# The lead of a fused attention and mixture-of-experts kernel: the first block's loads and work issued ahead of all later ones, six more staging places, four products of a block in one place

## The chip, the cores and the metric

The kernel runs on one NeuronCore of a Trainium2 chip. The metric is the device time of one launch in microseconds (us), the median of several runs. The engines are named as in the profile: PE (TensorE, matrix products and transposes), DVE (VectorE), ACT (ScalarE), POOL (GpSimd) and SP (SyncE), which in this kernel issues every DMA. Each engine works through its own instructions strictly in the order in which the program lists them.

## The reference

Pooled attention feeds a mixture of four experts, and that feeds a gated pair of products:

```
# q, k, v: (4, 8, 576, 64); 8 keys (values) are averaged to one: 72 per head
k_p = k.reshape(B, H, Sp, pool, D).mean(axis=3)
v_p = v.reshape(B, H, Sp, pool, D).mean(axis=3)
scores = scale * np.matmul(q, k_p.transpose(0, 1, 3, 2))
scores = scores - np.max(scores, axis=-1, keepdims=True)
attn = np.exp(scores)
attn = attn / (np.sum(attn, axis=-1, keepdims=True) + 1e-09)
attn_out = np.matmul(attn, v_p)                 # -> x: (2304, 512)
# experts, E = 4, p = normalised domain_probs
out += p[:, e:e + 1] * (np.maximum(x @ w1[e], 0.0) @ w2[e])
# tail
h = (x @ w1) * (x @ w2) @ w3;  result = h @ w_out
```

All of it is in float32; the big products are made of three products of a high and a low part of each operand.

## The kernel before

**Blocks and tiles.** The 2304 tokens are 18 tiles of 128 rows (t) and 6 blocks of 384 (i). Attention works by tile, the experts by block. The expert part is a sequence of units: unit n of expert 0 and block 0 makes one of 8 chunks of the hidden layer (`expert_h`: 12 products called `g<-xl,w1h`, `g<-xh,w1l`, `g<-xh,w1h` in the profile), and two units later its second product follows (`g<-hhl,w2h` and so on). Attention for blocks 1 to 5 is spread between the units: `hooks[n]` is a list of pieces, and `between(n)` runs it after the first (even n) or the second (odd n) half of a unit.

**The lead.** Before unit 0 stands the list `lead`: everything that block 0 needs. In it, `do_k(0)` pools the keys of batch 0 (`kp` on DVE, `kb` on POOL), `do_qT(t)` transposes the queries of tiles 0 to 2 on PE, `do_scores` and `do_exps` make the exponentials `e`, `do_normalise` divides them (on POOL for tiles 0 and 1), `do_v(0, ...)` pools the values of the 8 heads (three POOL additions for a head, except head 2, which DVE does), `do_turn` transposes the attention weights (`at_ps`, copied by ACT), and `do_attend(0)` is four pieces, hp = 0 to 3, each making two heads of x (`x_ps`), which ACT and DVE split into `xh` and `xl`. `warm(n)` is n transposes without use. `k1` and `kT1` stand for the pooling and the transposition of the keys of batch 1, which tile 4 is the first to need.

**Loads and places.** A load of q, k or v needs a staging place (`spots`); there are 14 of the kind "one", cut out of the tiles `stxh` and `stxl`, of which the six in `lead_only` are used once and the others come back when their content is used up, and two of the kind "wide", for queries of later tiles (`load_qb`, 4 or 8 DMAs for a tile). The list `loads` holds all loads in the order of their use. `fetch()` goes through it and issues each load for which a place is free, passing over those that find none; it runs before every piece. Weights come through a stream of four buffers, `raw`. All these DMAs stand in one queue, SP's, in the order of issue. `dp` is a table of 2304 x 4 numbers that is loaded in pieces of 16 bytes.

**Banks.** In the lead, PSUM banks are taken in turn from eight; afterwards `bank` alternates between two, q2 and q3, for scores, transposes and the like, and `g1_bank` between q0 and q1, for the first products of the experts and, in blocks 1 to 5, for `x_ps`.

Of the kernel before, what the change touches and what calls it, by code (L numbers as in the profile page):

```python
# [8 lines left out]
F32 = mybir.dt.float32  # L9
# [8 lines left out]
def fused_kernel(  # L18
# [24 lines left out]
    B, H, S, D = q.shape  # L43
# [3 lines left out]
    E, _, F = moe_w1.shape  # L47
    P = 128
# [3 lines left out]
    TPB = BLK // P  # L52
# [4 lines left out]
    NP = H // 2  # L57
    NROW = H * NK
    NCH = (NROW + P - 1) // P
# [4 lines left out]
    def segments(t0, n):  # L64
        done = 0
        while done < n:
            b, s = divmod(t0 + done, S)
            step = min(n - done, S - s)
            yield done, step, b, s
            done += step  # L70

    LAG = 2
    LEAD = 3
# [6 lines left out]
    acc_a = experts.enter_context(tc.tile_pool(name="acc_a", bufs=NB // 2))  # L80
# [10 lines left out]
    def bank_q(n, name):  # L91
        return ps_q.tile([P, 512], F32, tag=f"q{n}", name=name)
# [6 lines left out]
    def g1_bank(name):  # L99
        g1_turn[0] += 1  # L100
        return bank_q(g1_turn[0] % 2, name)[:, :BLK]
# [14 lines left out]
    def hi_lo(hi, lo, src, lo_eng=None):  # L116
        nc.scalar.activation(hi, src, AF.Copy)  # L117
        (lo_eng or nc.vector).tensor_tensor(lo, src, hi.bitcast(F32), op=ALU.subtract)  # L118
# [146 lines left out]
    with tc.manual_schedule():  # L265
# [12 lines left out]
        def bank(name):  # L278
            turn[0] += 1
            return spare[(turn[0] - 1) % len(spare)](name)  # L280
# [10 lines left out]


        staging = [xpool.tile([P, 3, 512], F32, tag=t, name="st" + t) for _ in range(3) for t in ("xh", "xl")]
        lead_only = [st[:, n, :] for st in staging[4:] for n in range(3)]
        spots = {"wide": [st[:, :2, :] for st in staging[:2]],
                 "one": lead_only + [st[:, n, :] for st in staging[2:4] for n in range(3)] + [st[:, 2, :] for st in staging[:2]]}
        holds = {}
# [1 line left out]
        def kind_of(what):  # L299
            return "wide" if what[0] == "qb" else "one"  # L300
# [75 lines left out]
        def make_qT(t):  # L376

            if t < LEAD:
                r = in_t.pop(("q", t))
                pt = bank("qT_ps")  # L380
                for hp in range(NP):
                    nc.tensor.transpose(pt[:, hp * P:(hp + 1) * P], r[:, hp * P:(hp + 1) * P], ident)
                qT = acc_a.tile([P, NP, P], F32, tag="acc", name="qT")
                nc.scalar.activation(qT.rearrange("p a b -> p (a b)"), pt, AF.Copy)
            else:
                qT = ap.tile([P, NP, P], F32, tag="qT", name="qT", bufs=1)
                nc.vector.transpose(qT.rearrange("p h (j a) -> p h a j", a=4), in_t.pop(("qb", t)))
            qT_t[t] = qT
# [50 lines left out]
        def attend(i, hp):  # L439
            if hp == 0:  # L440
                x_t[i] = tuple(xpool.tile([P, KC, BLK], F32R, tag=t, name=t) for t in ("xh", "xl"))
            xh, xl = x_t[i]
            px = g1_bank("x_ps") if i else bank("x_ps")
            for off, n, b, s in segments(i * BLK, BLK):
                for a in range(2):
                    nc.tensor.matmul(px[a * D:(a + 1) * D, off:off + n], vp_t[b][:NK, 2 * hp + a],  # L446
                                     at_t[i, hp // 2][:NK, 2 * (hp % 2) + a, off:off + n], start=True, stop=True)
            hi_lo(xh[:, hp, :], xl[:, hp, :], px[:, :BLK])

        loads = []  # L450

        def fetch():
            for what in list(loads):
                if spots[kind_of(what)]:
                    loads.remove(what)
                    {"q": load_q, "qb": load_qb, "k": load_k, "v": load_v}[what[0]](*what[1:])
# [7 lines left out]
        def do_k(b):  # L464
            return [(("k", b, c), lambda c=c: pool_k(b, c)) for c in range(NCH)]

        def do_kT(b):
            return [(None, lambda: make_kT(b, 0, 4)), (None, lambda: make_kT(b, 4, NCH))]
# [4 lines left out]
        def do_qT(t):  # L473
            return [(("q" if t < LEAD else "qb", t), lambda: make_qT(t))] if t < NTILE else []

        def do_scores(t):
            return [(None, lambda: scores(t))]

        def do_exps(t):
            return [(None, lambda: exps(t))]  # L480
# [4 lines left out]
        def do_turn(t):  # L485
            return [(None, lambda half=half: attn_T(t, half)) for half in range(2)]

        def do_attend(i):
            return [(None, lambda hp=hp: attend(i, hp)) for hp in range(NP)]
# [15 lines left out]
        def weight(eng):  # L505
            return [(None, lambda: stream.split(eng))]

        VE, GP = nc.vector, nc.gpsimd
        W0, W1, W2 = 14, 20, 14

        def warm(n):

            def f():
                pw = bank("warm")
                for _ in range(n):
                    nc.tensor.transpose(pw[:, :P], ident, ident)
            return [(None, f)]

        k0, kT0, k1, kT1 = do_k(0), do_kT(0), do_k(1), do_kT(1)
        v0 = do_v(0, GP, GP, VE, GP, GP, GP, GP, GP)  # L520
        lead = (warm(W0) + k0[:4] + kT0[:1] + k0[4:] + do_qT(0) + kT0[1:] + do_qT(1) + do_scores(0) + do_exps(0) + v0[:2]
                + do_qT(2) + do_scores(1) + v0[2:3] + do_exps(1) + do_scores(2) + v0[3:5] + do_normalise(0) + do_exps(2)
                + v0[5:6] + do_normalise(1) + warm(W1) + do_turn(0) + do_normalise(2, VE) + v0[6:]
                + warm(W2) + do_turn(1) + weight(GP) + k1[:2] + do_turn(2) + do_qT(3) + do_attend(0) + weight(VE))

        hooks = [[] for _ in range(2 * FC * ATT_BLOCKS + 4)]
        hooks[0] = k1[2:]
        hooks[1] = do_qT(TPB + 1)
        hooks[2] = kT1
        hooks[3] = [(None, probs)]  # L530
        hooks[5] = [(None, probs_T)]
        for t in range(TPB, NTILE + 1):
            h = hooks[3 * (t - TPB) + (t > TPB):]
            if t < NTILE:
                h[0] += do_scores(t) + do_exps(t)
                if t > TPB:
                    h[1] += do_qT(t + 1)
                one, two = do_normalise(t)
                h[1].append(one)
                h[2].append(two)  # L540
            if t > TPB:
                one, two = do_turn(t - 1)
                h[1].insert(0, one)
                h[2].insert(0, two)
                if t % TPB == 0:
                    for n, piece in enumerate(do_attend(t // TPB - 1)):
                        h[2 + n].append(piece)
        for b, at_v, at_k in ((1, 3, None), (2, 15, 11), (3, 26, 23)):
            for n, piece in enumerate(do_v(b, GP)):
                hooks[at_v + n].append(piece)  # L550
            if at_k:
                for n, piece in enumerate(do_k(b)):
                    hooks[at_k + n // 2].append(piece)
                hooks[at_k + 4] += do_kT(b)
        loads += [what for what, _ in lead + sum(hooks, []) if what]


        acc_t, x2_t, p_t = {}, {}, {}
# [316 lines left out]
                    add_w1(0, m)  # L875
            add_w2(0, n)
        dp = ap.tile([P, NTILE, E], F32, tag="dp", name="dp", bufs=1)
        fetch()
        stream.fill()
        nc.sync.dma_start(dp, domain_probs.rearrange("(t p) e -> p t e", p=P))  # L880
        for piece in lead:
# [71 lines left out]
        for half in range(2):  # L953
            for b in range(B):
# [24 lines left out]
                first, second = xo_t[0], xo_t[1]  # L979
# [95 lines left out]
```

## Time and profile before

| what | value |
|---|---|
| median of 3 runs | 1238.67 us (1236.69 to 1238.8) |
| profiled execution: span | 1235.0 us |
| PE busy | 1207.5 us (98%) |
| DVE, POOL, ACT busy | 666.8, 369.0, 276.3 us |
| DMA over the span | 137.28 MB on SP's queue, 112 GB/s on average |

The span is what the trace covers, from the first instruction to the last; the device time of a run has some microseconds more around it. The busy shares are averages over very different stages: the first 53 us, where block 0 is prepared, look nothing like the rest.

### The profile page before, as it was taken

To read this page: it belongs to the slowest core of one execution; us is meant where nothing else is said; L and a number is where in the kernel's file an instruction comes from. 1 tells how busy PE (TensorE), PEld (TensorE's weight loads), DVE (VectorE), ACT (ScalarE), POOL (GpSimd) and SP (SyncE) were. 2 spreads that over 40 slices of the span, in tenths; PEclk is the share of its full clock that TensorE was granted. 3 is DMA by queue.
4 is the path that set the end of the run, shared out by engine and by line. 5 is a ranking of instruction groups with operands and counts; after the bars stand their busy time and mean duration, and the time that the engine had idled before them with its cause. 6 is when DMAs were issued, how large, how long until landed. Compare 5 with 4: busy or idle time off the path is not lost.

```text
span 1235.0 us, 18786 instructions
## 1 busy us (share of the span) xinstructions
PE 1207.5 (98%) x7089; PEld 1151.8 (93%) x7089; DVE 666.8 (54%) x1489; ACT 276.3 (22%) x535; POOL 369.0 (30%) x432
## 2 busy tenths in 40 slices
PE   6899999999999999999999999999998999999997
PEld 5788898999999999999999999999987999999996
DVE  5777543444445446544434544444288778775453
ACT  3343331122111113111112211111253332231010
POOL 4664410034222117322124622112422222342111
PEclk9899999999999999999999999999999999999998
DMA  7853101134122235322114422222365343944642
GB/s 186 200 154 113 53 11 46 58 111 128 58 48 59 58 74 149 77 48 52 48 51 121 131 71 65 84 84 88 90 208 214 123 172 130 352 152 179 219 153 68
DMA packets 147758, 138.47 MB, mean 112 GB/s; under 512 B 48524, under 2 KB 114644, under 8 KB 147668
## 3 DMA queue, kind: packets, MB, share of 16 engines
q1 hardware_dynamic: 147668, 137.28, 36.6%
q8 instruction: 55, 0.90, 0.3%
q14 instruction: 35, 0.29, 0.1%
HBM read 96.05 MB, written 41.19 MB: 111 GB/s over the span
## 4 chain that ended last, share of the span: by engine, by line
PE 87%; DVE 5%; DMA 3%; issue 1%; POOL 1%; ACT 1%; SPq 1%; DVEq 0%; POOLq 0%; ACTq 0%
PE g L112 23%; PE g L113 23%; PE g L114 23%; PE s L112 5%; PE s L114 5%; PE s L113 5%; PE x_ps L446 1%; PE at_ps L434 1%; PE sc L400 1%; DMA stxl<-in_v_dram 1%; DVE w3hl L118 1%; DVE kp L332 1%; DMA stxh<-in_v_dram 1%; DVE s L651 1%; DMA half<-half 0%
## 5 line engine op out<-in xcount | busy, mean ns | idle before, releaser
L572 DVE SCALAR_TENSOR_TENSOR hhl<-g,hhh 128x384 fp32r<-128x384 f32 x192 | 106.6, 555 | 361.0 <-ACT hhh L571 360.9
L112 PE MATMUL g<-xl,w1h 128*128 128x384 f32 x768 | 262.4, 342 | 0.0
L113 PE MATMUL g<-xh,w1l 128*128 128x384 f32 x768 | 260.7, 339 | 0.0
L112 PE MATMUL g<-hhl,w2h 128*128 128x384 f32 x768 | 260.2, 339 | 0.2 <-DVE part L592 0.2
L114 PE MATMUL g<-xh,w1h 128*128 128x384 f32 x768 | 260.2, 339 | 0.0
L113 PE MATMUL g<-hhh,w2l 128*128 128x384 f32 x768 | 258.1, 336 | 0.0
L114 PE MATMUL g<-hhh,w2h 128*128 128x384 f32 x768 | 258.1, 336 | 0.0
L571 ACT ACTIVATE hhh<-g 128x384 fp32r<-128x384 f32 x192 | 94.4, 492 | 580.2 <-PE g L114 539.4
L224 POOL TENSOR_TENSOR dtmp<-dtmp 128x256 f32<-128x256 f32 x80 | 58.9, 736 | 408.4 <-DVE dtmp L223 365.2
L112 PEld LDWEIGHTS g<-xl,w1h 128*128 128x128 f32 x768 | 145.1, 189 | 4.9 <-issue 2.0
L112 PEld LDWEIGHTS g<-hhl,w2h 128*128 128x128 f32 x768 | 144.3, 188 | 5.0 <-issue 4.0
L113 PEld LDWEIGHTS g<-xh,w1l 128*128 128x128 f32 x768 | 145.0, 189 | 0.0
L114 PEld LDWEIGHTS g<-xh,w1h 128*128 128x128 f32 x768 | 144.9, 189 | 0.0
L113 PEld LDWEIGHTS g<-hhh,w2l 128*128 128x128 f32 x768 | 144.5, 188 | 0.0
L114 PEld LDWEIGHTS g<-hhh,w2h 128*128 128x128 f32 x768 | 144.2, 188 | 0.0
L118 POOL TENSOR_TENSOR g<-c,g 128x576 fp32r<-128x576 f32 x32 | 47.4, 1481 | 193.7 <-ACT g L117 178.2
L593 POOL TENSOR_TENSOR acc<-acc,part 128x384 f32<-128x384 f32 x72 | 71.1, 1019 | 72.0 <-DVE part L592 72.0
L112 PE MATMUL s<-xol,wh 128*128 128x288 f32 x308 | 91.2, 296 | 0.0
L114 PE MATMUL s<-xoh,wh 128*128 128x288 f32 x308 | 91.1, 296 | 0.0
L113 PE MATMUL s<-xoh,wl 128*128 128x288 f32 x308 | 90.6, 294 | 0.0
L112 PEld LDWEIGHTS s<-xol,wh 128*128 128x128 f32 x308 | 57.9, 188 | 0.4 <-DVE half L1011 0.2
L113 PEld LDWEIGHTS s<-xoh,wl 128*128 128x128 f32 x308 | 57.9, 188 | 0.2
(141 smaller groups left out, 1756.8 us busy)
## 6 DMA issues: line engine op xcount, KB each, us to landing
raw<-in_moe_w_dram SPq DMA_DIRECT2D x64, 256.0 KB
din<-in_moe_w_dram SPq DMA_DIRECT2D x64, 256.0 KB
p<-p SPq DMA_DIRECT2D x24, 192.0 KB
acc<-acc SPq DMA_DIRECT2D x6, 768.0 KB
xr<-acc SPq DMA_DIRECT2D x16, 288.0 KB
half<-ob SPq DMA_DIRECT2D x18, 256.0 KB
half<-half SPq DMA_DIRECT2D x18, 256.0 KB
out_dram<-half SPq DMA_DIRECT2D x18, 256.0 KB
```

The costliest lines, as they stand in the source:

```text
L112: nc.tensor.matmul(ps, lh, rl, start=first, stop=False)
L113: nc.tensor.matmul(ps, ll, rh, start=False, stop=False)
L114: nc.tensor.matmul(ps, lh, rh, start=False, stop=last)
L118: (lo_eng or nc.vector).tensor_tensor(lo, src, hi.bitcast(F32), op=ALU.subtract)
L224: nc.gpsimd.tensor_tensor(a, a, b, op=ALU.add)
L332: nc.vector.tensor_reduce(kp[:n], r[:n, :].rearrange("p (r d) -> p d r", d=D), axis=AX.X, op=ALU.add)
L400: nc.tensor.matmul(sc[off:off + n, (hp % 2) * W:(hp % 2 + 1) * W], qT[:, hp, off:off + n], kT_t[b][:, hp * W:(hp + 1) * W], start=True, st ...
L434: nc.tensor.transpose(pt[:NK, g * P:(g + 1) * P], e[:, half * G + g, :], ident)
L446: nc.tensor.matmul(px[a * D:(a + 1) * D, off:off + n], vp_t[b][:NK, 2 * hp + a], at_t[i, hp // 2][:NK, 2 * (hp % 2) + a, off:off + n], sta ...
L571: nc.scalar.activation(hh, ps, AF.Relu)
L572: nc.vector.scalar_tensor_tensor(hl, ps, 0.0, hh.bitcast(F32), op0=ALU.max, op1=ALU.subtract)
L593: nc.gpsimd.tensor_tensor(acc_t[i][:, c], acc_t[i][:, c], part, op=ALU.add)
```

## The change

It has five parts. (1) `first` lists block 0's own loads, and they stand ahead of all others in `loads`; the first `fetch` issues only these. (2) Three tiles of the pool that later holds the experts' sums lend six more places (`stacc`); the third tile holds the transposed queries of tiles 0 to 2. (3) The first two pooling pieces of batch 1's keys and the transposition of tile 3's queries move behind `do_attend(0)` and a weight split. (4) The other three pooling pieces move from `hooks[0]`, where they stood ahead of tile 3's scores, to `hooks[1]`; the last transposition of those keys goes from `hooks[2]` to `hooks[3]`. (5) A later block's four `attend` pieces, one in each of four hooks, stand together in `h[3]`, and the first two of them take their bank from `bank`.

```diff
+        acc_lead = [acc_a.tile([P, 3, 512], F32, tag="acc", name="stacc") for _ in range(3)]
-        lead_only = [st[:, n, :] for st in staging[4:] for n in range(3)]
+        lead_only = [st[:, n, :] for st in staging[4:] + acc_lead[1:] for n in range(3)]
...
-                qT = acc_a.tile([P, NP, P], F32, tag="acc", name="qT")
+                qT = acc_lead[0][:, t, :].rearrange("p (a b) -> p a b", b=P)
...
-            px = g1_bank("x_ps") if i else bank("x_ps")
+            px = g1_bank("x_ps") if i and hp >= 2 else bank("x_ps")
...
-        def fetch():
-            for what in list(loads):
+        def fetch(most=None):
+            for what in loads[:most]:
...
-                + warm(W2) + do_turn(1) + weight(GP) + k1[:2] + do_turn(2) + do_qT(3) + do_attend(0) + weight(VE))
+                + warm(W2) + do_turn(1) + weight(GP) + do_turn(2) + do_attend(0) + weight(VE) + k1[:2] + do_qT(3))
...
-        hooks[0] = k1[2:]
-        hooks[1] = do_qT(TPB + 1)
-        hooks[2] = kT1
-        hooks[3] = [(None, probs)]
+        hooks[1] = k1[2:] + do_qT(TPB + 1)
+        hooks[2] = kT1[:1]
+        hooks[3] = kT1[1:] + [(None, probs)]
...
-                    for n, piece in enumerate(do_attend(t // TPB - 1)):
-                        h[2 + n].append(piece)
+                    h[3] += do_attend(t // TPB - 1)
...
-        loads += [what for what, _ in lead + sum(hooks, []) if what]
+        first = [("k", 0, c) for c in range(NCH)] + [("q", t) for t in range(LEAD)] + [("v", 0, h) for h in range(H)]
+        loads += first + [what for what, _ in lead + sum(hooks, []) if what and what not in first]
...
-        fetch()
+        fetch(len(first))
```

The lists below show the order of instructions on three engines. On SP, from the start of the program, before (`in_k`, `in_q`, `in_v` are the inputs; a q tile is 128x8x64, a tile of later queries 4 times 32x4x224 or 8 times 16x4x224):

```order
L317 DMA stxl<-in_k_dram 64x512
L360 DMA stxl<-in_q_dram 128x8x64
L360 DMA stxh<-in_q_dram 128x8x64
L322 DMA stxh<-in_v_dram 72x512 x2
L360 DMA stxl<-in_q_dram 128x8x64
L322 DMA stxl<-in_v_dram 72x512 x2
L322 DMA stxh<-in_v_dram 72x512
L322 DMA stxl<-in_v_dram 72x512
L372 DMA stxh<-in_q_dram 32x4x224 x4
L372 DMA stxl<-in_q_dram 16x4x224 x8
L137 DMA raw<-in_moe_w_dram 128x4x128 x3
L135 DMA raw<-in_moe_w_dram 128x512
```

Behind these stand `dp`, the values of heads 6 and 7 and the keys of batch 1. And with the change, from the same row on:

```order
L318 DMA stxl<-in_k_dram 64x512
L361 DMA stxl<-in_q_dram 128x8x64
L361 DMA stacc<-in_q_dram 128x8x64 x2
L323 DMA stacc<-in_v_dram 72x512 x4
L323 DMA stxh<-in_v_dram 72x512 x3
L323 DMA stxl<-in_v_dram 72x512
L137 DMA raw<-in_moe_w_dram 128x4x128 x3
L135 DMA raw<-in_moe_w_dram 128x512
L880 DMA dp<-in_moe_domain_probs_dram 128x18x4
L318 DMA stxl<-in_k_dram 128x512 x2
L373 DMA stxh<-in_q_dram 32x4x224 x4
L318 DMA stxh<-in_k_dram 128x512
```

All eight heads' values now stand ahead of the 12 DMAs of later queries, the four weight buffers and `dp`; tile 2's queries went from behind the second head to ahead of the first, and the keys of batch 1 stay behind `dp`.

On DVE, from the end of the lead to tile 3's exponentials (`kp` pools keys of batch 1, `qT` is tile 3's transposition, `xl` and `w1l` the low parts of x and of a weight, `hhl` that of a unit's hidden chunk, `mx` and `e` the maximum and difference of tile 3's scores), before:

```order
L332 TENSOR_REDUCE kp<-stxh 128x64
L332 TENSOR_REDUCE kp<-stxl 128x64
L387 STREAM_TRANSPOSE qT<-stxh 128x4x4x32
L118 TENSOR_TENSOR xl<-x_ps,xh 128x384 x4
L118 TENSOR_TENSOR w1l<-raw,w1h 128x512
L572 SCALAR_TENSOR_TENSOR hhl<-g_433,hhh 128x384
L118 TENSOR_TENSOR w1l<-raw,w1h 128x512
L332 TENSOR_REDUCE kp<-stxl 128x64 x2
L332 TENSOR_REDUCE kp<-stxh 64x64
L412 TENSOR_REDUCE mx<-sc 128x4
L413 TENSOR_TENSOR e<-sc,mx 128x288
```

and with the change:

```order
L118 TENSOR_TENSOR xl<-x_ps,xh 128x384 x4
L118 TENSOR_TENSOR w1l<-raw,w1h 128x512
L333 TENSOR_REDUCE kp<-stxl 128x64 x2
L388 STREAM_TRANSPOSE qT<-stxh 128x4x4x32
L572 SCALAR_TENSOR_TENSOR hhl<-g_429,hhh 128x384
L118 TENSOR_TENSOR w1l<-raw,w1h 128x512
L413 TENSOR_REDUCE mx<-sc 128x4
L414 TENSOR_TENSOR e<-sc,mx 128x288
L413 TENSOR_REDUCE mx<-sc 128x4
L414 TENSOR_TENSOR e<-sc,mx 128x288
L333 TENSOR_REDUCE kp<-stxh 128x64
L333 TENSOR_REDUCE kp<-stxl 128x64
```

The same instructions stand there; two poolings and tile 3's transposition went from ahead of `xl` to behind the weight split, three poolings from ahead of tile 3's scores to behind them.

On ACT, where block 1's x is made some six units later (`xh` is x's high part, `at` the copied attention weights, g_949 and g_963 the hidden chunk of the same unit), before:

```order
L117 ACTIVATE xh<-x_ps 128x384 x2
L414 ACTIVATE e<-e 128x288 x2
L571 ACTIVATE hhh<-g_949 128x384
L117 ACTIVATE w2h<-raw 128x512
L437 ACTIVATE at<-at_ps 72x4x128
L117 ACTIVATE xh<-x_ps 128x384
L437 ACTIVATE at<-at_ps 72x4x128
L117 ACTIVATE xh<-x_ps 128x384
```

and with the change:

```order
L117 ACTIVATE xh<-x_ps 128x384 x4
L415 ACTIVATE e<-e 128x288 x2
L571 ACTIVATE hhh<-g_963 128x384
L117 ACTIVATE w2h<-raw 128x512
L438 ACTIVATE at<-at_ps 72x4x128 x2
```

The four pieces follow one another without other work between them, ahead of the next tile's exponentials.

## Rows read from the trace of the kernel before

**Rows 1.** The page: busy time of the engines.

```profile
PE 1207.5 (98%) x7089; PEld 1151.8 (93%) x7089; DVE 666.8 (54%) x1489; ACT 276.3 (22%) x535; POOL 369.0 (30%) x432
```

**Rows 2.** Windows: start:end, length, busy PE, PEld, DVE, ACT, POOL; clock, DMA share, GB/s.

```profile
0.00:30.20 30.20, 20.71 (x125) 16.38 (x125) 15.62 (x29) 11.50 (x22) 13.79 (x33) 1.00 0.78 182
30.20:37.10 6.90, 5.85 (x13) 3.42 (x14) 5.39 (x8) 1.01 (x2) 4.16 (x9) 0.51 0.93 236
...
43.90:47.30 3.40, 3.27 (x13) 2.96 (x12) 3.33 (x7) 2.53 (x7) 1.04 (x1) 0.50 0.67 171
...
53.00:240.00 187.00, 186.16 (x1150) 169.63 (x1149) 104.88 (x217) 58.99 (x123) 63.25 (x104) 1.00 0.28 80
```

**Rows 3.** Timeline of PE: start, duration, work, [idle before, releaser].

```profile
14.32 0.66 PE L382 MATMUL qT_ps<-ident,stxl 128*128 128x128 f32 x4 [0.63 <-DMA stxl<-in_q_dram]
...
23.37 2.19 PE L434 MATMUL at_ps<-ident,e 128*72 128x128 f32 x16 [0.18 <-POOL e L425]
26.17 2.16 PE L446 MATMUL x_ps<-at,vp 72*64 72x384 f32 x12 [0.61 <-ACT at L437]
31.18 3.15 PE L446 MATMUL x_ps<-at,vp 72*64 72x384 f32 x4 [2.86 <-POOL vp L355]
34.26 0.69 PE L112 MATMUL g<-xl,w1h 128*128 128x384 f32 x1
...
37.75 1.14 PE L400 MATMUL sc<-kT,qT 128*128 128x144 f32 x8
...
43.52 1.30 PE L341 MATMUL kT_ps<-ident,kb 128*128 128x128 f32 x5 [2.52 <-DVE e L413]
44.48 0.67 PE L112 MATMUL g<-xl,w1h 128*128 128x384 f32 x1
...
51.95 0.60 PE L434 MATMUL at_ps<-ident,e 128*72 128x128 f32 x4 [0.41 <-DVE e L413]
```

**Rows 4.** Timeline of SP's DMA issues: start, time until the last is issued, transfer.

```profile
15.10 5.28 SPq L372 DMA_DIRECT2D stxl<-in_q_dram  x8
...
22.54 0.43 SPq L880 DMA_DIRECT2D dp<-in_moe_domain_probs_dram  x1
23.09 3.77 SPq L322 DMA_DIRECT2D stxh<-in_v_dram  x2
```

**Rows 5.** Timeline of POOL: values of heads 0, 3, tile 1's division, head 6, one key product.

```profile
11.62 0.72 POOL L353 TENSOR_TENSOR stxh<-stxh 72x256 f32<-72x256 f32 x1 [1.20 <-DMA stxh<-in_v_dram]
...
16.15 0.72 POOL L353 TENSOR_TENSOR stxl<-stxl 72x256 f32<-72x256 f32 x1 [1.28 <-DMA stxl<-in_v_dram]
...
22.17 1.15 POOL L425 TENSOR_TENSOR e<-e,sm 128x576 f32<-128x576 f32 x1
29.49 0.72 POOL L353 TENSOR_TENSOR stxh<-stxh 72x256 f32<-72x256 f32 x1 [6.17 <-DMA stxh<-in_v_dram]
...
41.69 0.40 POOL L333 TENSOR_TENSOR kb<-kp,mk 128x128 f32<-128x128 f32 x1 [0.49 <-DVE kp L332]
```

**Rows 6.** Timeline of DVE: from head 2's values to tile 3's exponentials.

```profile
15.11 1.04 DVE L351 TENSOR_REDUCE vp<-stxl 72x64 f32<-72x512 f32 x1 [0.19 <-DMA stxl<-in_v_dram]
...
30.71 1.02 DVE L332 TENSOR_REDUCE kp<-stxh 128x64 f32<-128x512 f32 x1 [6.34 <-DMA stxh<-in_k_dram]
...
33.53 1.92 DVE L118 TENSOR_TENSOR xl<-x_ps,xh 128x384 fp32r<-128x384 f32 x4
...
38.47 0.56 DVE L572 SCALAR_TENSOR_TENSOR hhl<-g,hhh 128x384 fp32r<-128x384 f32 x1 [2.37 <-ACT hhh L571]
...
42.45 0.44 DVE L412 TENSOR_REDUCE mx<-sc 128x4 f32<-128x288 f32 x1
...
43.78 0.46 DVE L413 TENSOR_TENSOR e<-sc,mx 128x288 f32<-128x288 f32 x1
```

**Rows 7.** Timeline of DVE, where block 1's first two parts of x are split.

```profile
74.22 0.55 DVE L118 TENSOR_TENSOR xl<-x_ps,xh 128x384 fp32r<-128x384 f32 x1
74.69 2.03 DVE L332 TENSOR_REDUCE kp<-stxh 128x64 f32<-128x512 f32 x2
```

## The prediction, made before the run

> **What bounds the kernel now.** I read the page first: PE is busy 98% of the span [rows 1], so time can only be won where PE stands idle or runs slowly. The windows show where that is [rows 2]: up to 30.2 us PE works 20.71 us (much of it warming up), and from 53 to 240 us it idles only 0.84 of 187 us. So a microsecond saved before 53 us is kept, and one saved later has nearly nothing to come from. In the timeline of PE three things stand out in the lead [rows 3]: the last of four products for x (`x_ps`) waits 2.86 us for pooled values; the first product of unit 0 starts at 34.26; and the transposition of batch 1's keys waits 2.52 us. After either wait the granted clock falls to half (0.51 from 30.2 to 37.1, 0.50 from 43.9 to 47.3), which is 1.2 GHz [rows 2].
>
> The first wait leads to SP. POOL stands idle 6.17 us until head 6 lands, at 29.49 [rows 5]. Its DMA was issued at 23.09, behind the 12 DMAs of later queries (the last 8 alone took 5.28 us to issue), the weights and `dp` [rows 4].
>
> The second wait is put down to DVE's difference `e` [rows 3]. DVE works without a stop from 38.47 to 44.24 (43.78 + 0.46) [rows 6], and the keys' transposition needs the banks that tile 3's scores hold until then. So between the last `xl` (33.53 + 1.92 = 35.45) and 44.24 it is DVE's list of work, not PE, that sets the pace. At 51.95 PE once more waits 0.41 us for an `e` [rows 3].
>
> **The change, part by part.** *The lead up to x.* Heads 6 and 7 now stand right behind head 5. Head 3 lands at 16.15 and head 2 was in use at 15.11 [rows 5, 6], so a head takes about 1.04 us, and heads 4 to 7 are in by some 20.3. POOL then sets the start of x. From head 0 (11.62) to the end of tile 1's division (22.17 + 1.15 = 23.32) it needed 11.70 us, 1.28 of them idle for head 3 [rows 5]: 10.42 us of work, five heads at 1.62 and two divisions.
>
> But tile 2's queries now land ahead of head 0. Before, head 1 and these queries took from 11.62 to 14.32 together, 2.70 us [rows 3, 5]; a head takes 0.79 (14.32 to 15.11 [rows 3, 6]) to 1.04, so the queries cost 1.66 to 1.91. I take 1.9: head 0 at 13.5, the division's end at 23.92, 0.6 later than before. The bounds: if the queries cost nothing, POOL waits for head 3 as before (23.32); if head 0 comes only when the queries came, 14.32, the end is 24.74.
>
> PE began x 2.85 us after the division (26.17 against 23.32) and needs 0.72 for each pair of heads (2.16 for three) [rows 3]: start 26.77, end 29.65 instead of 34.33. Heads 6 and 7 are pooled by 23.92 + 2 x 1.62 = 27.2, and the fourth product needs them at 28.93, so that wait is gone with 1.7 us to spare. The last `xl` ended 1.12 us after the last product (35.45 against 34.33 [rows 3, 6]): now 30.77, 4.68 earlier. The first weight's low part, which POOL makes behind head 7, takes about as long as a division, so it is there by 28.5.
>
> *From x to tile 3.* Here something is given back. The two poolings and the transposition of tile 3, which DVE did while it waited for x (30.71 to 33.53, 2.82 us [rows 6]), now come behind `xl`. DVE needed 8.79 us from 35.45 to 44.24, of which 2.37 were a wait for unit 0's `hhh` [rows 6]. That wait is filled: 8.79 - 2.37 + 2.82 = 9.24, so the three poolings that are now last end at 30.77 + 9.24 = 40.01, and DVE is **4.23 us** ahead of before (44.24).
>
> The new wait is at tile 3's scores: their transposition ends about 0.65 (a weight split) + 2.82 after 30.77, at 34.2, while unit 0's 12 products, begun at 29.65, last at most the 3.49 us they took at half clock (34.26 to 37.75 [rows 3]). PE idles 1.1 us or more; behind it stand the products of units 1 and 2. Nobody on DVE waits for these until DVE reaches unit 1's `hhl`, behind the poolings, so the wait is hidden under DVE's list; without that cover it would cost its 1.1 to 2.5 us. The order "scores before keys" moves no work, but the keys' transposition now waits for the last pooling and POOL's product of 0.40 [rows 5] instead of for `e`: 40.01 + 0.5 + 0.1 = 40.6 for unit 2's first product, 3.9 ahead of 44.48. From there PE needed 7.06 us to the next stop (51.95 - 0.41) [rows 3]: 47.7. DVE, 4.23 ahead, releases that stop at 47.7 too. So 4.2 us are won at that point.
>
> *Loads behind.* The keys of batch 1 and tile 3's queries stand behind `dp`, as before; the first transfer behind it was in use 6.95 us after `dp` was issued (22.54 to 29.49 [rows 4, 5]). `dp` now has 12 DMAs fewer and two heads more ahead of it; without the 5.28 us of the last eight it goes out at about 17.3, and the first key is there at 24.3. At 1.04 a transfer, five more are in by 29.5, needed from 31.4 on. Hidden, with 2 us to spare at the first and more at the transposition.
>
> *Places* cost no instruction. *Four products in one place:* PE issues four pairs in 2.88 us and DVE splits each in 0.48 (1.92 for four) [rows 3, 6]. The scores behind them take the first pair's bank, free 0.72 + 1.12 = 1.84 after the start, so 1.04 us before it is wanted; unit n+1 takes the third pair's, free at 3.28 and wanted at 2.88 + 1.14 = 4.02. In block 1 two poolings (2.03) now stand ahead of the first `xl`, not behind it [rows 7]; they run under the unit's second product. I take nothing; the bound is 2.03 - 0.74 = 1.3 us there, and there is no more than 0.84 us of idle time to win [rows 2].
>
> **Sum.** 1235.0 - 4.2 = 1230.8 us of span. The median of the runs is 3.67 us above the profiled span; I leave that as it is: **1234.5 us**. The bounds of head 0 make it 4.8 (23.32) to 3.4 (24.74): 1233.9 to 1235.3.
>
> **A rule against it.** The change makes one long wait into two: 1.1 us or more ahead of tile 3's scores and, with unit 1's 12 products behind them, one of 2 us or more ahead of the keys. The rows show half clock after each of the two waits of before, and each time full clock again after a stretch of dense products [rows 2, 3]. If the clock came back one such low stretch (3.4 us, 43.9 to 47.3) later than before, products that took 1.7 at 2.4 GHz would take 3.4, and DVE covers only 0.1 of it: 1236.1. The Trainium skill ("TensorE: Matmul & The Clock Gate", section "Why this matters for your kernels") advises against idle gaps between bursts of products, since the array falls to the slow clock after them. By that rule the new gap is a loss; in the trace the slow stretches lie where DVE sets the pace, so I expect most of it to be covered.
>
> **Rivals.**
> - *Head 0 is not delayed*: 4.8 us, 1233.9. For it: the queries and the heads overlap on 16 DMA engines. Against: POOL waited 1.20 us for head 0 [rows 5], so landing sets it.
> - *The clock comes back later*: 1236.1, as above.
> - *The gain is given back to DMA*: the lead's loads must come 4.2 us sooner, and the DMA engines are busy 0.93 of the time from 30.2 to 37.1 and 0.78 before [rows 2]. If the keys or tile 3's queries reach DVE 2 to 4 us after it wants them, its list of 9.24 ends as much later, and 2.2 to 0.2 us are left: 1236.5 to 1238.5. Against: from 43.9 on the share is 0.67, and raw weights wait for buffers, not for the engines.
> - *Slower*: the four products in one place. DVE takes its work in order; where `xl` comes more than 1.04 us late, scores wait, then the unit. At 1.34 us in each of five blocks, 6.7 us, the kernel is 2.5 slower: 1241.2 or more. From 0.84 a block the gain is gone. Against: DVE is busy 104.88 of 187 us there [rows 2], and only block 1 has poolings ahead.
>
> **Chances.** 2.5 us (0.2%) is about what can be told from no change. The forecast 0.60, head 0 undelayed 0.12, clock 0.08, DMA 0.14, slower 0.06. Faster: the first two and half of the third, 0.76; the same 0.18; slower 0.06. Range 1232.4 to 1237.4: the forecast's bounds and the clock, with the 2.1 us by which the three runs differ. It leaves out the slow rival and most of the DMA one.
>
> **What will show it.** Right: no wait of POOL for heads 6 and 7; the four products of x within 3 us, without a stop, ending near 29.7; `xl` ending near 30.8; a wait of PE ahead of tile 3's scores; the keys' transposition near 40; PE's idle time after 53 us unchanged. Wrong: head 0 in use before 12 or after 14.5; DVE waiting for keys or queries between 31 and 40; low clock beyond 47; idle PE ahead of scores behind the grouped products.

## The result, and the profile after

The changed kernel takes 1226.91 us in the median of 4 runs (1226.71 to 1228.87); the kernel before, run beside it, 1237.68 (1235.6 to 1238.8). The ratio is 0.9919, with a 95% interval of 0.9907 to 0.9931: 10.8 us faster. The forecast was 1234.5 us, 4.2 below the 1238.67 known then, and the measured time lies outside its range (1232.4 to 1237.4). The profiled span is 1225.0 us against 1235.0, so the two traces can account for 10.0 of it.

The lead after, in the timeline of PE (columns as in [rows 3]):

```profile
23.03 1.07 PE L435 MATMUL at_ps<-ident,e 128*72 128x128 f32 x8 [0.18 <-POOL e L426]
...
25.83 2.80 PE L447 MATMUL x_ps<-at,vp 72*64 72x384 f32 x16 [0.37 <-ACT at L438]
28.56 0.45 PE L112 MATMUL g<-xl,w1h 128*128 128x384 f32 x1
...
33.39 1.25 PE L401 MATMUL sc<-kT,qT 128*128 128x144 f32 x8 [2.49 <-DVE qT L388]
...
39.69 0.33 PE L342 MATMUL kT_ps<-ident,kb 128*128 128x128 f32 x1 [0.59 <-POOL kb L334]
39.78 0.42 PE L112 MATMUL g<-xl,w1h 128*128 128x384 f32 x1
...
46.68 0.60 PE L435 MATMUL at_ps<-ident,e 128*72 128x128 f32 x4 [1.17 <-DVE e L414]
```

Against [rows 3], unit 0 begins at 28.56 instead of 34.26, unit 2 at 39.78 instead of 44.48, and the stop ahead of the attention weights ends at 46.68 instead of 51.95. The wait for pooled values is gone; the new one of 2.49 us stands ahead of tile 3's scores. On POOL and DVE:

```profile
12.61 0.72 POOL L354 TENSOR_TENSOR stacc<-stacc 72x256 f32<-72x256 f32 x1 [2.22 <-DMA stacc<-in_v_dram]
...
21.82 1.15 POOL L426 TENSOR_TENSOR e<-e,sm 128x576 f32<-128x576 f32 x1
22.93 0.72 POOL L354 TENSOR_TENSOR stxh<-stxh 72x256 f32<-72x256 f32 x1
```

```profile
27.26 2.52 DVE L118 TENSOR_TENSOR xl<-x_ps,xh 128x384 fp32r<-128x384 f32 x4 [3.00 <-ACT xh L117]
29.75 0.69 DVE L118 TENSOR_TENSOR w1l<-raw,w1h 128x512 fp32r<-128x512 f32 x1
...
38.15 1.02 DVE L333 TENSOR_REDUCE kp<-stxh 64x64 f32<-64x512 f32 x1
```

From 12.61 on POOL has no idle time until head 7; head 6 follows the division without a wait, where it waited 6.17 us [rows 5]. DVE idles 3.00 us ahead of `xl` and then works through its list, which ends at 39.17 (38.15 + 1.02).

The windows of after, with the columns of [rows 2]:

```profile
30.20:37.10 6.90, 4.41 (x22) 4.09 (x21) 6.83 (x11) 2.42 (x5) 2.03 (x3) 0.81 0.78 221
37.10:43.90 6.80, 6.04 (x42) 5.14 (x41) 6.70 (x11) 3.71 (x8) 4.91 (x7) 0.94 0.79 135
43.90:47.30 3.40, 2.21 (x14) 1.66 (x12) 3.26 (x9) 0.44 (x1) 3.13 (x5) 1.00 0.75 226
...
53.00:240.00 187.00, 185.52 (x1175) 175.86 (x1174) 107.29 (x228) 58.75 (x119) 60.90 (x99) 1.00 0.27 78
```

There is one stretch of half clock in the lead where before had two [rows 2]. It lies between 34 and 38 us (the first two windows share it, hence 0.81 and 0.94), and DVE works on its list meanwhile without a stop. From 53 us on, PE's idle time is 1.48 of 187 us; it did not fall (0.84 in [rows 2]), and 0.54 of it is one wait of a unit for `xl` behind block 5's grouped products. Yet the number of products in that window rose from 1150 to 1175, and the busy time of the weight loads (the second figure, PEld) from 169.63 to 175.86. The lead over before is 5.3 us at 46.68 and 9.6 at the start of the last scores (163.85 against 173.47): nearly as much again was won where PE already looked full.

Where it came from is seen where block 1's x is made (`at_ps` is the transposition of attention weights). Before, a pair of heads stood alone in each of four places, here the first:

```profile
71.68 0.60 PE L434 MATMUL at_ps<-ident,e 128*72 128x128 f32 x4
72.21 0.87 PE L446 MATMUL x_ps<-at,vp 72*64 72x192 f32 x8
73.01 0.45 PE L112 MATMUL g<-hhl,w2h 128*128 128x384 f32 x1
```

And with the change:

```profile
66.33 0.60 PE L435 MATMUL at_ps<-ident,e 128*72 128x128 f32 x4
66.68 0.42 PE L112 MATMUL g<-hhl,w2h 128*128 128x384 f32 x1
...
68.94 2.82 PE L447 MATMUL x_ps<-at,vp 72*64 72x192 f32 x32
71.69 1.25 PE L401 MATMUL sc<-kT,qT 128*128 128x144 f32 x8
```

Starts must be read here, not durations, since the durations of neighbours overlap: the four products for x hold PE for 2.75 us (68.94 to 71.69), 0.69 for each pair of heads, and the transposition for 0.35. Before, it was 0.80 for the pair (72.21 to 73.01) and 0.53 for the transposition (71.68 to 72.21). Read in this way over blocks 1 to 5, the products for x hold PE for 15.86 us before and 14.20 after (with the wait of 0.54), and 13 transpositions that stood just ahead of such a place lost 0.17 us each. That is about 3.9 of the 4.3 us won behind 46.68.

### The profile page after: what moved, and what is told of

Same layout as the page of the kernel before. It is cut to its first block, busy times and chain, and to the rows that moved or that the text cites. A ratio compares the mean times of both kernels' runs of the same rounds, so it can differ in the third digit from the quotient of the medians.

```text
span 1225.0 us, 18777 instructions
## 1 busy us (share of the span) xinstructions
PE 1198.9 (98%) x7089; PEld 1152.3 (94%) x7089; DVE 667.6 (54%) x1489; ACT 277.6 (23%) x535; POOL 369.3 (30%) x432
## 4 chain that ended last, share of the span: by engine, by line
PE 90%; DVE 4%; DMA 2%; POOL 1%; issue 1%; ACT 1%; SPq 1%; DVEq 0%; POOLq 0%; ACTq 0%
PE g L113 24%; PE g L114 24%; PE g L112 24%; PE s L112 5%; PE s L114 5%; PE s L113 5%; PE x_ps L447 1%; PE at_ps L435 1%; PE sc L401 1%; DVE w3hl L118 1%; DMA raw<-w 1%; DMA half<-half 0%; POOL w2l L118 0%; DMA stacc<-in_v_dram 0%; DVE kp L333 0%
## 5 line engine op out<-in xcount | busy, mean ns | idle before, releaser
L117 ACT ACTIVATE g<-c 128x576 fp32r<-128x576 f32 x32 | 21.9, 686 | 160.5 <-DVE c L947 160.5
```

## The experiments

Medians are of 4 to 6 runs. Runs of the kernel before stand beside each group of experiments, on the same chip; their medians go from 1236.3 to 1238.3 us, so a difference of under 1 us between kernels of different groups says little. A "place" is a spot in the order where products for x stand together, and a theory's letter is that of the expectation above it.

**Part 5 undone.** Four places again, all with `g1_bank`:

```diff
-            px = g1_bank("x_ps") if i and hp >= 2 else bank("x_ps")
+            px = g1_bank("x_ps") if i else bank("x_ps")
...
-                    h[3] += do_attend(t // TPB - 1)
+                    for n, piece in enumerate(do_attend(t // TPB - 1)):
+                        h[2 + n].append(piece)
```

> The changed kernel with its fifth part alone undone: the four products of a block stand in four hooks again, all with banks of g1_bank. In the traces before and after, the lead is 5.3 us ahead at 53 us and the end is 10.0 ahead. Theory A: the other 4.7 us come from PE's own time for the products of x, which cost more where each stands alone between products of another kind; then this kernel takes about 1226.9 + 4.7 = 1231.6 us, with PE's idle time after 53 us as in the changed kernel. Theory B: they come from the lead too (later work runs with more room because it began earlier); then it takes about 1227 us.

Measured: 1231.32 us (1230.35 to 1231.91), ratio 0.9948 [0.9936, 0.9961]. Theory A: 4.4 us of the gain are part 5. Block 1 in its trace, first PE, then the weight loads (PEld) of the same place:

```profile
66.54 0.60 PE L435 MATMUL at_ps<-ident,e 128*72 128x128 f32 x4
67.06 0.87 PE L447 MATMUL x_ps<-at,vp 72*64 72x192 f32 x8
67.86 0.44 PE L112 MATMUL g<-hhl,w2h 128*128 128x384 f32 x1
```

```profile
66.37 0.50 PEld L435 LDWEIGHTS at_ps<-ident,e 128*72 128x72 f32 x4
67.06 0.52 PEld L447 LDWEIGHTS x_ps<-at,vp 72*64 72x64 f32 x8 [0.20 <-issue]
67.86 0.19 PEld L112 LDWEIGHTS g<-hhl,w2h 128*128 128x128 f32 x1 [0.28 <-issue]
67.97 0.19 PEld L113 LDWEIGHTS g<-hhh,w2l 128*128 128x128 f32 x1
```

The transposition now holds PE 0.52 us instead of 0.35, and one pair of heads 0.80 instead of 0.69. The cause is in the loads: those of the transposition begin at 66.37, ahead of its products (66.54), under the work before. Those of x begin only with x's own first product, after 0.20 us without a load, and the next unit's after 0.28. Nothing that the profile shows is waited for ("issue"). The page "TensorEngine Tiling (Array Packing)" of the Trainium skill, section "Key Properties", says that a change of the array's tiling mode drains the engine. The trace agrees with such a drain, though none is seen in it as such: x's products use 64 columns of the array, their neighbours 72 or 128, and a place costs about 0.3 us, in and out together.

That 64 columns suffice for it, without the 72 rows of x's products, is seen in the changed kernel at tile 4's scores, which have 128 rows and 64 columns. Their loads have a gap ahead and one behind as well, while the transposition between two units (128 rows, 72 columns, at 66.33) has none on either side:

```profile
42.03 0.93 PEld L401 LDWEIGHTS sc<-kT,qT 128*64 128x64 f32 x16 [0.25 <-issue]
43.16 0.19 PEld L112 LDWEIGHTS g<-hhl,w2h 128*128 128x128 f32 x1 [0.20 <-issue]
```

**Part 5 alone**, on the kernel before.

> The kernel before with the fifth part alone: a block's four products in one place, two of them with banks of the other pair. Theory A (products of x cost PE less in one place): about 1237.7 - 4.7 = 1233.0 us, the lead unchanged, unit 0 starting near 34.3. Theory B (all comes from the lead): about 1237.7 us.

Measured: 1232.62 us (1231.52 to 1233.24), ratio 0.9959 [0.9947, 0.9972]. Theory A again: 5.0 us.

**Two places**, first with all banks from `g1_bank`, then with one of each kind (`if i and hp % 2`):

```diff
-            px = g1_bank("x_ps") if i and hp >= 2 else bank("x_ps")
+            px = g1_bank("x_ps") if i else bank("x_ps")
...
-                    h[3] += do_attend(t // TPB - 1)
+                    four = do_attend(t // TPB - 1)
+                    h[3] += four[:2]
+                    h[4] += four[2:]
```

> The changed kernel with the four products for x in two places, two in h[3] and two in h[4]; all are still behind the transpositions of the attention weights. Theory A (each place where products for x begin and end costs PE a fixed time: 15 places fewer gave 5.0 us on the kernel before and 4.4 us on the changed one, 0.29 to 0.33 a place): five places more cost 1.5 to 1.7 us, 1228.4 to 1228.6. Rival B (the gain is that the products no longer stand next to transpositions of attention weights whose copies they wait for; how many places there are does not matter): 1226.9.

> Two places again (h[3] and h[4]), but in each the first product for x takes its bank from bank and the second from g1_bank, so that neither waits for a bank that the unit before has just filled. Theory A (a place costs PE about 0.35 us: 0.15 behind the products for x, 0.1 ahead of them, 0.1 in the next group; the rest of what the first version with two places lost were waits for banks, 0.54 to 0.65 us each in its trace): five places more cost 1.75 us, 1228.7. Rival B (two places lose whatever the banks are): 1231.9, as there.

Measured: 1231.93 us (1231.49 to 1232.67), then 1229.42 (1228.12 to 1229.82), ratio 0.994 [0.9927, 0.9954]. The first missed both forecasts: 5.0 us lost for five places. Its trace shows waits of PE inside the places (up to 0.44 us, for the bank that the unit before had just filled) and behind them (0.54, for `xl`). With other banks half of the loss is gone. The 2.5 us that stay are more than theory A's 1.75: 0.5 a place, of which part is again a wait (0.36 us of scores for `xl` in block 1). So a place has a price, and banks have another.

**One product between.** A transposition without use ahead of the second, third and fourth product for x:

```diff
+            if i and hp:
+                nc.tensor.transpose(px[:, :P], ident, ident)
```

> The changed kernel with one transposition without use (128x128) ahead of the second, third and fourth product for x, in the same bank, in each of the five later blocks: 15 transpositions more, nothing else moved. By itself a transposition takes 0.09 to 0.11 us where many follow one another: 15 are 1.4 to 1.7 us. Theory A (going over between 128-row products and the 72-row, 64-column products for x costs 0.29 to 0.33 us there and back): 15 times 0.3 more, and the 15 themselves hide partly in it: 1230.5 to 1233. Rival B (only the neighbourhood of the waits matters): 1228.3 to 1228.6.

Measured: 1233.53 us (1232.54 to 1234.21), 6.6 more than without, 0.44 for each; that is a little above theory A's range (1230.5 to 1233) and far from B's. Nothing else moved, and no engine is waited for in the group:

```profile
68.41 0.87 PE L449 MATMUL x_ps<-at,vp 72*64 72x192 f32 x8
69.21 0.33 PE L446 MATMUL x_ps<-ident 128*128 128x128 f32 x1
69.47 0.87 PE L449 MATMUL x_ps<-at,vp 72*64 72x192 f32 x8
...
72.39 1.25 PE L401 MATMUL sc<-kT,qT 128*128 128x144 f32 x8
```

From the first start to the scores it is 3.98 us instead of 2.75. A pair takes 0.80 again, and the lone transposition 0.26 (69.21 to 69.47), where the 14 in a row that warm PE up follow one another every 0.11. The five groups of the kernel hold PE for 19.95 us instead of 14.20, which is the difference between the two spans (1230.8 against 1225.0). This is the plainest test: the change of product shape alone costs the time.

**One place, all banks from `g1_bank`.**

```diff
-            px = g1_bank("x_ps") if i and hp >= 2 else bank("x_ps")
+            px = g1_bank("x_ps") if i else bank("x_ps")
```

> The changed kernel with its four products in one place, but all four in the two banks of g1_bank. Theory A (the two banks from bank are what keeps the place free of waits): the second product waits some 0.65 us for the bank of the unit before, the third and fourth each for the low part of the product two before, 1.84 us after that one began and so 0.4 us or more late: 1.3 us a block or more, five blocks 6.5 us, 1233.4. Rival B (ACT and DVE keep up; only the first wait, 0.65 us a block): 1230.2.

Measured: 1232.47 us (1231.51 to 1235.67): 5.6 lost, theory A, though the waits fall otherwise. In block 1 the second product does not wait; the third does:

```profile
69.50 1.52 PE L447 MATMUL x_ps<-at,vp 72*64 72x192 f32 x16
72.06 1.52 PE L447 MATMUL x_ps<-at,vp 72*64 72x192 f32 x16 [1.04 <-DVE xl L118]
```

In the other blocks waits of 0.38 to 0.54 us stand inside the group. The five groups hold PE for 19.80 us instead of 14.20, all of the loss. That is close to what the prediction's slower rival would have cost (1.34 a block), by waits inside the group and not behind it; the two banks from `bank` are what keeps it away.

**Loads and places alone** (parts 3, 4 and 5 undone).

> The changed kernel with parts three, four and five undone, so that only the order of loads and the places are new: the keys of batch 1 are pooled, and tile 3's queries transposed, ahead of x's low parts on DVE. In the trace after, DVE stands idle for 3.0 us ahead of these low parts, the keys land by 25.4 and tile 3's queries by 27.4. Theory A: two poolings and the transposition fill that idle time; the low parts end some 0.6 later (30.4) but 2.98 us of DVE's list are gone, so the lead is about 2.4 us shorter than after's: 1237.7 - 5.3 - 2.4 = 1230.0 us. Theory C: moving them behind x is what made the lead shorter, since loads behind dp come late; then the lead gains less than 5.3 and the time is over 1232.4.

Measured: 1229.48 us (1228.91 to 1231.29), ratio 0.9932 [0.9918, 0.9946], theory A: 8.1 us by parts 1 and 2. With parts 3 and 4 added (the first experiment) it was 1231.32: these two cost 1.8.

**Parts 3 and 4 undone, one at a time and together**, with part 5 kept:

```diff
-                ... + do_turn(2) + do_attend(0) + weight(VE) + k1[:2] + do_qT(3))
+                ... + k1[:2] + do_turn(2) + do_qT(3) + do_attend(0) + weight(VE))
...
-        hooks[1] = k1[2:] + do_qT(TPB + 1)
-        hooks[2] = kT1[:1]
-        hooks[3] = kT1[1:] + [(None, probs)]
+        hooks[0] = k1[2:]
+        hooks[1] = do_qT(TPB + 1)
+        hooks[2] = kT1
+        hooks[3] = [(None, probs)]
```

> The changed kernel with its third part alone undone: two poolings and tile 3's transposition ahead of x again. Theory A (they fill DVE's idle time ahead of x): about 1226.9 - 2.4 = 1224.5 us, and PE's wait ahead of tile 3's scores is gone. Theory C (the loads come too late for that): x waits for them, 1227 us or more.

> The changed kernel with part 4 alone undone: the last three poolings of batch 1's keys stand ahead of tile 3's scores again, and both pieces of the keys' transposition in hooks[2]. Part 3 alone was worth -0.8 us (1226.1 with it undone against 1226.9). If parts 3 and 4 each cost by themselves and add up to the 1.8 us that they cost together (1231.3 against 1229.5), part 4 costs about 1.0: 1225.9. If part 4 is what pays for part 3 (tile 3's scores need not wait for three poolings), undoing it alone loses: the scores' maximum comes 3 us later on DVE, and of that at least 1 us ends in the time: 1228 or more.

> Parts 1, 2 and 5 alone: the changed kernel with parts 3 and 4 both undone. Theory A (with the products for x in four places, parts 3 and 4 together cost 1.8 us, 1231.3 against 1229.5; that is a loss of the lead and does not depend on part 5): 1225.1, the fastest so far but for held loads. Rival B (undone one at a time they gave 0.8 and -0.3; together they give the sum, 0.5): 1226.4. Rival C (keys ahead of x make PE wait for DVE's low part in some executions, and the gain is gone): 1227 or more.

Measured, part 3 undone: 1226.13 us (1225.7 to 1226.43), a third of theory A's gain. Part 4 undone: 1227.18 (1227.16 to 1228.79), between its two forecasts. Both undone: 1224.71 (1224.56 to 1226.09), ratio 0.989 [0.9875, 0.9904], theory A and the lowest median of all; the step from the loads alone (1229.48) to here is part 5 by itself once more, 4.8 us. PE and DVE of the last:

```profile
25.79 2.80 PE L447 MATMUL x_ps<-at,vp 72*64 72x384 f32 x16 [0.37 <-ACT at L438]
...
30.74 1.14 PE L401 MATMUL sc<-kT,qT 128*128 128x144 f32 x8
...
40.84 1.20 PE L401 MATMUL sc<-kT,qT 128*64 128x144 f32 x16 [1.06 <-ACT kT L344]
...
44.41 0.60 PE L435 MATMUL at_ps<-ident,e 128*72 128x128 f32 x4
```

```profile
24.15 2.02 DVE L333 TENSOR_REDUCE kp<-stxl 128x64 f32<-128x512 f32 x2
26.10 1.12 DVE L388 STREAM_TRANSPOSE qT<-stxh 128x512 f32<-128x512 f32 x1
27.22 2.52 DVE L118 TENSOR_TENSOR xl<-x_ps,xh 128x384 fp32r<-128x384 f32 x4
```

The two poolings and the transposition fill just the 3 us in which DVE otherwise waits for x, and tile 3's scores need not wait. The attention weights are turned at 44.41, 2.27 us before the changed kernel. What the prediction called given back is this, and it need not have been.

Why both together give more than the two singly is not tested. The traces differ in the clock: with part 3 alone undone, PE waited three times for keys (1.64, 0.61 and 0.44 us) and the granted clock was 0.50 from 36.55 to 43.4 us; with both undone it stayed at 1.00 from 33 to 42.

**The clock.** Part 3 alone undone, and 19 transpositions without use in PE's waits for keys:

```diff
             for c in range(g0, g1):
+                for _ in range({2: 12, 3: 4, 4: 3}.get(c, 0) if b == 1 else 0):
+                    nc.tensor.transpose(pt[:, (c - g0) * P:(c - g0 + 1) * P], ident, ident)
```

> The variant with part 3 alone undone (1226.1), with 19 transpositions without use put into PE's waits ahead of the third, fourth and fifth transposition of batch 1's keys (12, 4 and 3, each in the place that is overwritten behind it), so that PE is not idle from 34.1 to 37.6 us. Theory A (in that variant 1.9 us were lost because the granted clock was at 1.2 GHz from 36.6 to 43.4 and unit 2's products took 4.1 us in place of 2.2): clock at full, 1224.3. Rival B (DVE's list sets the pace behind the transposition anyway, so the half clock was hidden): 1226.1, or a few tenths more for transpositions that come too late.

Measured: 1228.43 us (1226.46 to 1228.96), not faster than without (1226.13). The granted clock stays at 1.00 from 34 to 46 us, and unit 2's products end at 40.38, but then PE waits. PE and ACT there:

```profile
43.25 1.20 PE L403 MATMUL sc<-kT,qT 128*64 128x144 f32 x16 [2.88 <-ACT kT L346]
```

```profile
42.08 0.63 ACT L117 ACTIVATE w2h<-raw 128x512 fp32r<-128x512 f32 x1 [4.24 <-DMA raw<-in_moe_w_dram]
42.62 0.75 ACT L346 ACTIVATE kT<-kT_ps 128x512 f32<-128x512 f32 x2
```

The keys' copy stands on ACT behind a weight that has not landed. My theory that the clock alone set the time of this variant falls: with the clock at full, PE waits for that load instead.

**The loads behind.** Everything behind the keys and tile 4's queries held back until the middle of unit 1 to let weights go first, with and without those transpositions (and part 3 undone):

> Keys early as in the variant with part 3 alone undone, the 19 transpositions without use in PE's waits for keys, and all loads behind batch 1's keys and tile 4's queries held back until the middle of unit 1, so that the weights of units 3 and 1 stand ahead of batch 1's values in SP's queue. Theory A (in the two variants before, the weight that ACT splits ahead of the keys' copy landed at 40.2 and 42.1 us, behind four loads of values and four of queries, and tile 4's scores waited for that copy): the weight lands some 2.5 us earlier, and with the clock kept at full the scores begin near 40.2 in place of 41.9: 1224.4. Rival B (DVE's maxima and differences or POOL's division of tile 3 set what follows): 1226.1. Rival C (the values come too late for POOL): 1227 or more.

> The same loads held back, without the 19 transpositions. If the half clock that followed PE's waits in the variant with part 3 alone undone sets the time once the weight is there, unit 2's products still end near 41.9: 1226.1. If the weight alone was the limit: 1224.4.

Measured: 1227.75 us (1226.4 to 1229.06) and 1225.82 (1225.13 to 1226.11). The second is as forecast by the half clock; the first agrees with C. Holding the values that long has a price: in the second POOL waited 4.20 us for the first of them, in use at 44.69, and PE then 0.73 us for POOL's division of tile 4:

```profile
53.96 0.63 PE L435 MATMUL at_ps<-ident,e 128*72 128x128 f32 x4 [0.73 <-POOL e L426]
```

In the first the values were in use at 45.46 and that wait was 1.3 us.

**`dp` later**, behind keys and queries: in the changed kernel, in the fastest variant, and there with loads held back until the second of unit 0's two hooks; the fastest with loads held back alone.

> The changed kernel as it is, with dp issued late alone. There the keys stand behind x, DVE never waits for them, and the early issue of dp is hidden: 1226.9. If the loads behind dp (weights of units 1 and 3 among them) set the lead after all: 1225.5 or less.

> The same with dp, the table loaded in pieces of 16 bytes, issued behind the keys of batch 1 and the queries of tiles 3 and 4 instead of ahead of them. In the traces so far the DMA behind dp takes 4.4 to 4.6 us to issue, and where the keys stand ahead of x, DVE waits 1.94 us for keys and queries (1.17, 0.15 and 0.62). Theory A (that issue time is what makes them late): no such wait, and up to 1.9 us less than without this edit: 1223.5 to 1225. Rival B (what is won there is lost where the weights behind come later): the same time as without this edit.

> Parts 1, 2 and 5, dp issued late, and all loads behind batch 1's keys and tile 4's queries held back until the middle of unit 0's pair of hooks, so that four weight loads stand ahead of batch 1's values. Theory A (with dp late x began 1.2 us earlier, 24.63, but tile 4's scores waited 4.06 us, until 42.64, because the weight that ACT splits ahead of the keys' copy landed at 41.45 behind values and queries): the weight lands before 36, the scores begin near 38.6, and 3 to 4 us of 1228.2 come back: 1224 to 1225. Rival B (DMA is busy throughout, what is moved back is missed elsewhere as much): 1228.

> Parts 1, 2 and 5 with the same loads held back, dp as in the changed kernel. There tile 4's scores waited 1.06 us for the copy behind that weight (landed 39.65). Theory A: that wait goes, 1223.7. Rival B: 1224.7 as without the edit, since DVE's maxima and differences stand at the same place (its stop ahead of the transposition of attention weights was 0.25 us).

Measured: 1225.9 us (1224.96 to 1227.68), too near to 1226.91 to tell its two cases apart; 1228.24 (1227.37 to 1229.24); 1224.88 (1224.71 to 1226.13); 1225.55 (1223.99 to 1226.26). The second was a clear miss, 3.5 us slower than 1224.71 where a gain was expected; the third got 3.4 of it back. PE's wait for the keys' copy in the second:

```profile
42.64 2.19 PE L401 MATMUL sc<-kT,qT 128*64 128x144 f32 x16 [4.06 <-ACT kT L344]
```

and the same scores in the third, with the stop that is then the last:

```profile
39.60 1.20 PE L401 MATMUL sc<-kT,qT 128*64 128x144 f32 x16
...
44.85 0.60 PE L435 MATMUL at_ps<-ident,e 128*72 128x128 f32 x4 [1.76 <-DVE e L414]
```

So the late weight, which ACT could split only from 41.47 on in the second, was the cause there. With `dp` early, letting that load go first gained nothing (1225.55 against 1224.71): the wait for the copy went, but the next stop still waits 0.30 us for DVE's difference, as rival B had it.

## Why the prediction was wrong

**The failed step: "Four products in one place: ... I take nothing".** This term of the sum, put at nothing, measured 5.0 us on the kernel before, 4.8 on the kernel with new loads alone and 4.4 on the whole. The prediction asked only whether grouping makes someone wait, and took PE's idle time of 0.84 us [rows 2] as all that could be won; its first paragraph says the same of everything behind 53 us. But what was won was inside PE's busy time: 15 places fewer, each with a change from products of 72 or 128 columns to those of 64 and back that leaves the weight load uncovered. The rows had a sign of it: PE busy 186.16 of 187 us, but the weight loads only 169.63 [rows 2]. The Trainium skill's page "Trainium Kernel Development and Optimization", section "Best Practices", says to judge the distance to the limit by the share of peak reached and the busy share of weight loads, and not by that of products; the trace agrees (loads 175.86 after, while PE busy went from 186.16 to 185.52).

**Head 0.** Expected at 13.5 (11.62 to 14.32), it came at 12.61, 0.99 us later than before and not 1.9. The 1.28 us in which POOL waited for head 3 [rows 5] were gone as well, so tile 1's division ended at 22.97, 0.35 earlier than before instead of 0.6 later. So the head cost 0.99 us where 1.9 were taken, and the rival "head 0 undelayed" was about as near as the forecast.

**From x to tile 3.** x began 2.86 us behind the division (2.85 taken) and ran without a stop; `xl` ended at 29.78 (30.77), nearly all of the difference the division's 0.95. DVE's list took 9.39 us (9.24). The wait ahead of tile 3's scores came, 2.49 us, and was hidden under that list; unit 2 began at 39.78 (40.6) and the stop ended at 46.68 (47.7). The mechanism held; the term of 4.2 us measured 5.3 in the traces. What was not seen is that the move of part 3, costed at 2.82 us on DVE against 2.37 of filled wait, loses 2.2 us with part 4, as DVE's 3 us ahead of `xl` go empty.

**The sum.** 5.3 in the lead and 4.4 to 5.0 from grouping make 9.7 to 10.3, against 10.0 between the spans and 10.8 between the medians. The chain of experiments, 8.1 (loads and places) - 1.8 (parts 3 and 4) + 4.4 (grouping), gives 10.7 by construction, since each step starts where the one before ends; it is the three measurements of grouping that check one another. Of the 7.6 us by which 1234.5 missed, 4.7 are the grouping in the spans, 1.1 the lead, and 1.8 a term that says nothing of the change: the sum kept 3.67 us between span and median, and the changed kernel's median is 1.9 above its profiled span.

**The clock.** The low stretch came earlier and not later as the rival had it, there was one and not two, and it was hidden: behind it PE still waited 0.16 and 0.59 us for keys. **DMA.** `dp` went out at 15.22 (17.3 taken) and DVE waited for no keys, as said; transfers were seen to set the pace only in variants where the keys are pooled earlier. **Slower by grouping.** The waits are real, but the choice of banks keeps them away, down to the one of 0.54 us in block 5: undoing it cost 5.6 us.

**Open.** What exactly PE does in the 0.20 and 0.28 us without a weight load is not shown, only that products of 64 columns next to wider ones bring them. The 19 transpositions without use made two variants 2 us slower, and that stays open in the main. In the traces 1.1 us of the one loss (spans of 1226.9 and 1224.0) and 0.6 of the other (1226.0 and 1224.2) stand at the last scores; the rest, 1.8 and 1.3, comes behind them, where the kernels compared do the same work.

## What to carry to other kernels

An engine that is busy all the time can still win time: compare the starts of neighbouring products, not their durations, and put products of one shape together, since each place of another shape cost some 0.3 us here, in and out together. Choose the banks with the order, for the same grouping with two banks in place of four gave all of it back. And before work is moved behind a wait, look whether it was what filled the wait of the engine that sets the pace.

## What was not expected of the hardware

- Going from the transposition (72 columns) to products of 64 columns cost PE 0.17 us (0.52 against 0.35), from a unit's products (128 columns) 0.10 (0.27 from 68.67 to 68.94, where they follow one another every 0.17), and coming back 0.15 (0.80 for one pair of heads, 2.75 for four, so 0.65 for each further one): 0.32 for a place behind such a transposition, and 0.29 to 0.33 by the times of the kernels. A single 128-column product between them cost 0.44.
- The DMA that is issued behind `dp` (pieces of 16 bytes) took 4.3 to 4.6 us to issue where `dp` stood at 15 to 16 us, 3.3 where it stood at 22.5, and 1.0 to 1.3 where it stood at 28 to 29. Why is not shown.
- Loads land differently from one execution to the next: with the same first loads and `dp` at 15 to 16 us, x began between 25.4 and 26.7 us in the profiled executions (24.6 to 25.7 in the three with `dp` late). The stretch from the last scores to the end differed by more, 1059.6 to 1062.2 us in kernels that do the same work there.
